# Gated linear attention and a cosine MLP in one kernel: four pairs' transposes moved to the DMA queue, and a new order of steps

## The chip, the cores and the metric

The kernel runs on one core of a Trainium2 chip. The metric is the device time of one execution in microseconds; lower is better. The engines in the profile are TensorE (PE, with its weight loads as PEld), VectorE (DVE), ScalarE (ACT), GpSimd (POOL) and SyncE (SP), which here only issues transfers; a name with q at its end (SPq, POOLq) is that engine's sequencer.

## The reference

Two layers follow each other. The first is a recurrence over 768 tokens, for 4 batches and 8 heads of width 48:

```python
for t in range(S):
    state = alpha[:, :, t, :, None] * state + np.einsum('bhd,bhe->bhde', k[:, :, t], v[:, :, t])
    y[:, :, t] = np.einsum('bhd,bhde->bhe', q[:, :, t], state)
x = y.transpose(0, 2, 1, 3).reshape(B * S, H * D)      # 3072 x 384
h = x @ w_in                                           # 384 x 2048
out = (h * np.cos(h)) @ w_out                          # 2048 x 384
```

Inputs and output are float32; the kernel computes its products in bfloat16.

## The kernel before

**Tiling.** The recurrence is computed in chunks. The 3072 tokens are cut into twelve blocks of 256 tokens, which the code calls J and this text a pair (each has two chunks of 128 tokens, c = 0 and 1; token parity is e). Three pairs make a batch, so the state starts anew at pairs 0, 3, 6 and 9. Within a pair, cumulative sums of log alpha give two factors: k is multiplied by the inverse of the running product and q by the product itself. After that the inner part is plain masked attention, and the state from earlier chunks is added.

**Steps of a pair.** `load a/k/q/v` bring the four inputs (384 KB each, on SP). `mula` multiplies the two tokens' alphas on POOL, `ln` takes logarithms on ACT, `cums` and `cums0` sum them on PE, `sub` is a subtraction on DVE, `icp` and `exps` are the exponentials on ACT; `eb` is all four exponentials of a pair with the next pair's `ln`. `sk` and `sq` scale k and q for one parity into the tiles kh and qh (on POOL, or on DVE where the order says `:D`). `castv` converts v on POOL, and `vst` stacks it into the tile vs with four SBUF-to-SBUF transfers of 64 KB on SP (L246); the first three pairs do that with `vpe` and `vev` on PE and ACT. `decay` prepares the chunk's decay on POOL. `trans` is 32 transposes on PE into PSUM (L288), and `evT` copies one chunk of them to the tile qkT in SBUF, on DVE or ACT (L294). `scores` (L303) are the products of k and q of one chunk, and `mask` (L309, DVE) masks them into SBUF. `outer` (L321), `add` (L335, DVE) and `state` (L343, POOL) update the state. `yT` (L370) forms the output of the pair, and `evy` (L379) copies a chunk of it to SBUF as xT.

**Steps of the MLP.** For each pair, `m1 u` (L390) is one of four steps of the first product: 12 matmuls of 256 columns into one two-bank PSUM tile. `sin u` (L396, ACT) is its cosine, `gate u` (L401, DVE) the product h cos h. The second stage is cut into parts: `m2 c part` (L419) is four matmuls of 384 columns into one PSUM bank, four parts make one chunk's 128 output rows. `evo` (L431) copies them to SBUF and `out` stores them from SP. The weights come in four quarters each, `w1 u` (L126) and `w2 u` (L132), cast to bfloat16 on the way and issued by POOL.

**Order.** Nothing is scheduled by the compiler: the table PLAN gives every step of every pair (the twelve columns) a number, and the program is emitted by these numbers. So each engine's queue is in the order of the table, and an engine that waits holds all that stands behind it on its queue; this is true of SP and of POOL, which issue transfers among other work. A colon and a letter after a number name the engine (D: DVE, A: ACT). IDLE lists dummy matmuls on PE, as (place, count).

**Buffers.** PSUM has three two-bank tiles named "h", which `cums0`, `vpe`, `trans`, `scores`, `outer`, `yT` and `m1` share; one bank "o" for `m2`, and one "x" for `cums`. In SBUF there are three buffers each for k, q, v, kh, qh, qkT, four for alpha, and two for vs. The ScalarE function table is loaded anew when exponentials and cosines alternate (nine times each way).

**Gate of the loads.** GATES makes the load of one input wait until a given step of TensorE is through. All loads that stand behind it on SP's queue wait as well:

```python
GATES, AFTER = {("a", 2): ("yT", 1)}, {}
```

Of the kernel before, what the change touches and what calls it, by code (L numbers as in the profile page):

```python
# [16 lines left out]
def kernel(  # L17
# [26 lines left out]
    NL, NQ, NV, NS = 4, 3, 3, 2  # L44
# [35 lines left out]
    for lst, nm, n in ((lna_t, "lna", NL), (kh_t, "kh", NQ), (qh_t, "qh", NQ), (vp_t, "vp", NV)):  # L80
        for r in range(n):
            t = consts.tile([C, 2, H, 64], BF, tag=f"{nm}{r}", name=f"{nm}{r}")
            nc.vector.memset(t[:, :, :, D:64], 0.0)
            lst.append(t)
# [14 lines left out]
    GATES, AFTER = {("a", 2): ("yT", 1)}, {}  # L99
# [7 lines left out]
    def load(nm, J):  # L107
        b, g = J // NJB, J % NJB
        t = sb.tile([C, H, 2, D], FP, tag=nm, name=nm, bufs=BUF["a" if nm == "a" else "in"])
        dma = nc.sync.dma_start(  # L110
# [120 lines left out]
    def scale_k(J, e, eng):  # L231
        icp_ = icp_sb.pop((J, e)).rearrange("p (h d) -> p h d", h=H)
        eng.tensor_tensor(out=kh_t[J % NQ][:, e, :, 0:D], in0=kqv["k", J][:, :, e], in1=icp_, op=ALU.mult)  # L233

    def scale_q(J, e, eng):
        cp = cp_sb[J, e][:, 0:HD].rearrange("p (h d) -> p h d", h=H)
        eng.tensor_tensor(out=qh_t[J % NQ][:, e, :, 0:D], in0=kqv["q", J][:, :, e], in1=cp, op=ALU.mult)  # L237
# [43 lines left out]
    def trans(J):  # L281
        T_ps[J] = ps.tile([C, 2, 2 * NP, 2, HC], BF, tag="h", name="T_ps", bufs=3)
        for i, x in ((1, kh_t[J % NQ]), (0, qh_t[J % NQ])):
            for p in range(NP):
                for e in range(2):
                    for c in range(2):
                        r = slice(HC * c, HC * c + HC)
                        last = nc.tensor.transpose(T_ps[J][:, c, i * NP + p, e, :],  # L288
                                            x[r, e, 2 * p : 2 * p + 2, :].rearrange("s h d -> s (h d)"), ident_bf[r, r])
# [23 lines left out]
    def outer(J):  # L313
# [3 lines left out]
        for p in range(NP):  # L317
            for e in range(2):
                for c in range(n):
# [3 lines left out]
                        kh[r, e, 2 * p : 2 * p + 2, :].rearrange("s h d -> s (h d)"),  # L323
# [61 lines left out]
    def mlp1(J, u):  # L385
        h_ps[J, u] = ps.tile([C, FW, T2], FP, tag="h", name="h_ps", bufs=3)
        for f in range(FW):
            ft = u * FW + f
            for kk in range(KT):
                nc.tensor.matmul(h_ps[J, u][:, f, :], w1[:, kk, ft * C : (ft + 1) * C], xT[J][:, kk, :],  # L390
                                 start=(kk == 0), stop=(kk == KT - 1))

# [15 lines left out]
    def mlp2(J, c, part):  # L408
# [8 lines left out]
        for o, cols in zip(o_ps[J, c], HALVES if last_tile else [slice(0, DM)]):  # L417
            for ft in fts:
                nc.tensor.matmul(o[:, 0 : cols.stop - cols.start], gsb[J][:, ft, c * C : (c + 1) * C], w2[:, ft, cols],  # L419
                                 start=(done == 1 and ft == fts[0]), stop=(done == MP and ft == fts[-1]))  # L420

# [19 lines left out]
    def idle(n):  # L441
# [5 lines left out]
    copies = {"DVE": nc.vector.tensor_copy, "ACT": nc.scalar.copy}  # L447
    mults = {"DVE": nc.vector, "POOL": nc.gpsimd}
    steps = {
        "load": lambda J, nm: load(nm, J), "w1": load_w1, "w2": load_w2,  # L450
# [4 lines left out]
        "evT": lambda J, c, eng="DVE": evict_T(J, c, copies[eng]), "scores": scores, "mask": mask, "outer": outer,  # L455
# [7 lines left out]
        "load a": "10 20 960 1030 1170 1450 1460 2230 2570 2290 3490 2960",  # L463
        "load k": "70 190 1040 1270 1530 2020 1990 3050 3500 4180 3440 4290",
        "load q": "100 230 300 1290 1620 1950 2580 2850 3980 4010 3970 4770",
        "load v": "40 290 1130 1220 1730 1930 1940 3090 3680 2990 4970 4850",
        "w1": "330 200 470 460 - - - - - - - -",
        "w2": "260 580 820 690 - - - - - - - -",
        "mula": "- - - 1090 1340 1790 2240 2480 3220 3070 3610 3820",
        "ln": "30 110 1060 1100 - - - - - - - -",  # L470
        "cums0": "50 160 1070 - - - - - - - - -",
        "cums": "140 210 1080 1120 1630 2130 2460 3140 3360 3830 4200 4660",
        "sub": "- - - 1200 1640 2140 2470 3150 3370 3840 4210 4950",
        "icp 0": "60 310 1180 - - - - - - - - -",
        "icp 1": "240 270 1330 - - - - - - - - -",
        "exps 0": "120 170 1140 - - - - - - - - -",
        "exps 1": "150 220 1230 - - - - - - - - -",
        "eb": "- - - 1430 1800 2250 2590 3230 3380 4150 4480 5190",
        "sk 0": "80:D 320 1190 1440 2180 2280 2940 3240 3650 4190 4490:D 5470",
        "sk 1": "250 280 1350:D 1560:D 2100 2260 2890:D 3340 3890 4510 4890 5480",  # L480
        "sq 0": "130:D 500:D 1150 1590 1910 2680 3130 3510 3990 4530 4800 5200",
        "sq 1": "340:D 510:D 1280:D 1670 1880 2270 2820 3530 4070 4520 4560 5450",
        "castv": "90 610 1210 1260 2120 2750 2720 3760 3730 4980 5000 5360",
        "vst": "- - - 1820 2320 3120 3110 4040 4450 5160 5010 5380",
        "vpe": "440 650 1540 - - - - - - - - -",
        "vev": "480:A 660:A 1580:A - - - - - - - - -",
        "decay": "180 730 1250 1470 2560 2450 3040 3810 3700 4780 4700 5210",
        "trans": "350 520 1360 1690 2190 2690 3160 3550 4350 4540 4900 5490",
        "evT 0": "370 590 1380 1840:A 2210 2700:A 3200 3710 4390:A 4550 4960:A 5500:A",
        "evT 1": "400:A 540 1520 1710 2380 2730 3180 3560 4420 4580 4910:A 5520",  # L490
        "scores 0": "380 600 1610 1890 2660 2830 3320 3960 4440 4930 5560 5760",
        "scores 1": "420 670 1570 1850 2390 3350 3480 4090 4460 5060 5080 5790",
        "mask 0": "410 640 1650 1900 2670 2860 3330 4000 4650 4940 5600 5770",
        "mask 1": "430 720 1600 1870 2420 3390 3540 4110 4470 5070 5100 5880",
        "outer": "360 680 1410 1700 2640 3170 3300 4120 4370 4990 5510 5780",
        "add 0": "390 710 1420 1720 2650 3190 3310 4130 4400 5040 5530 5840",
        "add 1": "620 760 - 1860 2800 - 3460 4250 - 5090 5700 -",
        "state 0": "450 750 1740 1810 2710 3400 3450 4140 4860 5050 5550 5960",
        "state 1": "630 990 - 2370 2810 - 3600 4360 - 5110 5830 -",
        "yT": "490 780 1750 2150 2790 3570 3620 4330 4870 5170 5670 5970",  # L500
        "evy 0": "530:D 790:D 1760:D 2160:D 2840:D 3590:D 3660:D 4380:D 4880 5180:D 5750 6030",
        "evy 1": "550 800 1770:D 2170:D 2900 3580 3630:D 4340 4920:D 5220:D 5710 6020",
        "m1 0": "740 940 2000 2520 2980 3670 3900 4620 5150 5610 5900 6040",
        "m1 1": "560 890 1960 2400 2950 3860 3750 4630 5250 5390 5850 6090",
        "m1 2": "860 920 2030 2310 3000 3690 4230 4710 5340 5930 6190 6290",
        "m1 3": "830 970 2050 2490 2910 3930 4080 4730 5580 5300 6230 6390",
        "sin 0": "770 1000 2010 2540 3010 3720 3910 4670 5230 5660 5910 6060",
        "sin 1": "570 900 1970 2410 2970 3870 3790 4690 5280 5400 5860 6100",
        "sin 2": "870 930 2040 2330 3080 3770 4270 4720 5350 5940 6200 6300",
        "sin 3": "840 1390 2060 2500 2920 4020 4220 4760 5620 5320 6240 6400",  # L510
        "gate 0": "810 1110 2070 2550 3030 3740 3920 4680 5240 5740 6070 6080",
        "gate 1": "700 910 1980 2440 3020 3880 3800 4740 5290 5420 5920 6110",
        "gate 2": "880 980 2110 2430 3210 3780 4280 4750 5370 5950 6210 6330",
        "gate 3": "850 1400 2340 2510 2930 4030 4260 4810 5630 5330 6310 6410",
        "m2 0 0": "1020 1490 2080 3060 3430 4310 4790 5410 5730 6130 6350 6510",
        "m2 0 1": "950 1480 2300 2880 3420 4170 4640 5270 5800 6140 6340 6540",
        "m2 0 2": "1050 1500 2200 2760 3470 4160 4820 5430 5810 6150 6360 6500",
        "m2 0 3": "1010 1510 2350 2770 3410 4300 4830 5440 5720 6120 6320 6550",
        "m2 1 0": "1300 1680 2610 3260 3950 4600 5030 5650 5980 6270 6420 6580",
        "m2 1 1": "1240 1780 2620 3280 4060 4430 5120 5570 6000 6250 6440 6590",  # L520
        "m2 1 2": "1310 1660 2600 3270 4050 4410 5130 5640 5990 6260 6460 6480",
        "m2 1 3": "1320 1830 2530 3250 3640 4570 5020 5590 5890 6220 6430 6490",
        "evo 0": "1160:D 1550 2360 3100:D 3520 4320 4840 5460 5820:D 6170 6370:D 6560",
        "evo 1": "1370:D 1920:D 2630:D 3290 4100:D 4610:D 5140:D 5680:D 6010:D 6280 6470:D 6600",
        "out 0": "2090 2780 3850 4590 3940 6160 5540 5870 6050 6180 6380 6570",
        "out 1": "2220 2740 2870 4500 4240 5310 5260 5690 6450 6520 6530 6610",
    }
    IDLE = [(45, 10), (155, 2), (345, 9), (375, 1), (435, 4), (485, 3)]
# [45 lines left out]
```

## Time and profile before

| | us |
|---|---|
| median of 3 runs (185.56 to 185.94) | 185.88 |
| the profiled execution | 185.78 |
| its span in the profile | 184.0 |
| TensorE busy | 173.0 (94% of the span) |
| VectorE busy | 134.5 (73%) |
| ScalarE busy | 124.9 (68%) |
| GpSimd busy | 83.5 (45%) |
| granted TensorE clock, mean | 0.999 |

All times are from one profiled execution. A group's line reads: line of the code, engine, operation, what it writes and reads, count, then busy time, mean duration in ns, and the idle time of the engine just before it with what ended that. The chain that ended last is followed back from the last instruction: each piece is what released the next one. A wait's line names who waited for whom, the total, how often and the longest. Landing times of single transfers are from the trace's DMA issues and the updates of their semaphores.

The first transfers of the execution were issued and landed as follows:

| transfer | queue | issued at | landed at |
|---|---|---|---|
| a, a, v, k, q, k, q (pairs 0 and 1) | SP | 0.74 to 7.21 | 4.41, 5.92, 7.43, 8.93, 10.44, 11.95, 13.41 |
| w1, step 1 | POOL | 8.55 | 15.30 |
| v of pair 1 | SP | 8.70 | 19.64 |
| q of pair 2 | SP | 10.18 | 26.43 |
| w1, steps 0, 3 and 2 | POOL | 13.99, 15.60, 16.40 | 22.15, 24.87, 27.10 |
| w2, first landed after that | POOL | 17.18 | 29.11 |
| a2, a3, k2, v2 | SP | 25.30 to 31.20 | 35.02, 36.32, 37.73, 39.07 |

### The profile page before, as it was taken

To read this page: it belongs to the slowest core of one execution; us is meant where nothing else is said; L and a number is where in the kernel's file an instruction comes from. 1 tells how busy PE (TensorE), PEld (TensorE's weight loads), DVE (VectorE), ACT (ScalarE), POOL (GpSimd) and SP (SyncE) were. 2 spreads that over 40 slices of the span, in tenths; PEclk is the share of its full clock that TensorE was granted. 3 is DMA by queue.
4 is the path that set the end of the run, shared out by engine and by line. 5 is a ranking of instruction groups with operands and counts; after the bars stand their busy time and mean duration, and the time that the engine had idled before them with its cause. 6 is when DMAs were issued, how large, how long until landed. Compare 5 with 4: busy or idle time off the path is not lost.

```text
span 184.0 us, 5742 instructions
## 1 busy us (share of the span) xinstructions
PE 173.0 (94%) x2457; PEld 125.5 (68%) x2458; DVE 134.5 (73%) x182; ACT 124.9 (68%) x157; POOL 83.5 (45%) x116
## 2 busy tenths in 40 slices
PE   7989579979999999999999999999899999999993
PEld 2445458646687776876787777876687677776672
DVE  7069777669999899799969898879587674734520
ACT  3745457789879999895978989869774517435201
POOL 5388550079883484939686093903901110000000
PEclk9999999999999999999999999999999999999999
DMA  6999999999999979963996579003420121010312
GB/s 146 261 248 224 216 202 206 262 256 257 261 213 262 304 170 278 260 164 85 278 289 154 140 215 245 18 6 88 143 71 4 41 88 51 0 43 4 127 44 86
DMA packets 60137, 29.47 MB, mean 160 GB/s; under 512 B 51024, under 2 KB 60112, under 8 KB 60112
## 3 DMA queue, kind: packets, MB, share of 16 engines
q1 hardware_dynamic: 56256, 25.86, 57.9%
q0 software_dynamic: 3712, 3.15, 10.6%
q8 instruction: 19, 0.31, 0.8%
q10 hardware_dynamic: 144, 0.10, 0.2%
q14 instruction: 6, 0.05, 0.1%
HBM read 25.17 MB, written 4.72 MB: 162 GB/s over the span
## 4 chain that ended last, share of the span: by engine, by line
PE 68%; DMA 11%; issue 7%; SPq 6%; POOL 5%; ACT 1%; DVE 1%; POOLq 0%; DVEq 0%
PE h_ps L390 28%; PE o_ps L419 26%; DMA v<-in_v_dram 6%; SPq L110 4%; PE y_ps L370 4%; DMA k<-in_k_dram 4%; PE A_ps L303 2%; PE T_ps L288 2%; PE U_ps L321 2%; SPq L246 2%; PE o_last L419 1%; DMA vs<-vp 1%; POOL un L343 1%; POOL a L154 1%; PE cums L168 1%
## 5 line engine op out<-in xcount | busy, mean ns | idle before, releaser
L401 DVE TENSOR_TENSOR gsb<-h_ps,c_sb 128x1024 bf16<-128x1024 f32 x48 | 58.4, 1222 | 20.0 <-ACT c_sb L396 18.8
L396 ACT ACTIVATE c_sb<-h_ps,halfpi 128x1024 bf16<-128x1024 f32 x48 | 53.4, 1114 | 28.5 <-PE h_ps L390 28.4
L390 PE MATMUL h_ps<-xT,w 128*128 128x256 bf16 x576 | 67.5, 273 | 0.7 <-DMA w<-in_moe_w_in_dram 0.5
L419 PE MATMUL o_ps<-w,gsb 128*128 128x384 bf16 x368 | 66.7, 326 | 0.0
L390 PEld LDWEIGHTS <-w 128*128 128x128 bf16 x576 | 55.4, 98 | 9.7 <-DMA w<-in_moe_w_in_dram 0.8
L419 PEld LDWEIGHTS <-gsb 128*128 128x128 bf16 x400 | 37.0, 98 | 20.8
L343 POOL TENSOR_TENSOR un<-us,c 128x384 bf16<-128x384 f32 x20 | 16.7, 836 | 33.1 <-DVE us L335 26.0
L309 DVE TENSOR_TENSOR A_sb<-A_ps,msk 128x1024 bf16<-128x1024 f32 x24 | 29.1, 1220 | 3.6 <-PE A_ps L303 3.4
L233 POOL TENSOR_TENSOR kh<-k,icp 128x384 bf16<-128x384 f32 x19 | 19.5, 1032 | 10.2 <-ACT lna L146 5.3
L237 POOL TENSOR_TENSOR qh<-q,cp 128x384 bf16<-128x384 f32 x19 | 18.8, 999 | 6.1 <-ACT cp L219 4.2
L154 POOL TENSOR_TENSOR a<-a 128x384 f32<-128x384 f32 x9 | 9.0, 997 | 11.8 <-DMA a<-in_alpha_dram 11.8
L240 POOL CAST vp<-v 128x768 bf16<-128x768 f32 x12 | 10.1, 853 | 6.4 <-DMA v<-in_v_dram 6.0
L146 ACT ACTIVATE lna<-a 128x768 bf16<-128x768 f32 x12 | 10.1, 842 | 4.1 <-DMA a<-in_alpha_dram 2.4
L141 ACT ACT_TABLE_LOAD x9 | 11.5, 1283 | 0.9 <-PEq L558 0.7
L294 DVE COPY qkT<-T_ps 128x1024 bf16<-128x1024 bf16 x17 | 11.4, 682 | 0.8 <-PE T_ps L288 0.8
L396 ACT ACT_TABLE_LOAD x9 | 11.5, 1283 | 0.2
L431 ACT COPY o_sb<-o_ps 128x384 f32<-128x384 f32 x10 | 4.8, 478 | 9.6 <-PE o_ps L419 9.6
L431 DVE COPY o_sb<-o_ps 128x384 f32<-128x384 f32 x13 | 7.2, 554 | 4.3 <-PE o_ps L419 4.2
L445 PE MATMUL idle_ps<-zeros 128*128 128x512 bf16 x28 | 9.0, 469 | 1.2 <-DVE halfpi L77 1.2
L379 DVE CAST xT<-y_ps 128x384 bf16<-128x384 f32 x14 | 7.7, 584 | 3.1 <-PE y_ps L370 2.9
L335 DVE TENSOR_TENSOR us<-U_ps,un 128x384 f32<-128x384 f32 x16 | 8.8, 551 | 1.3 <-PE U_ps L321 1.2
L303 PE MATMUL A_ps<-qkT 48*128 48x128 bf16 x192 | 8.7, 217 | 0.6 <-DVE qkT L294 0.5
(68 smaller groups left out, 149.2 us busy)
## 6 DMA issues: line engine op xcount, KB each, us to landing
a<-in_alpha_dram SPq DMA_DIRECT2D x12, 384.0 KB, 6.0
v<-in_v_dram SPq DMA_DIRECT2D x12, 384.0 KB, 6.1
k<-in_k_dram SPq DMA_DIRECT2D x12, 384.0 KB, 6.0
q<-in_q_dram SPq DMA_DIRECT2D x12, 384.0 KB, 6.2
out_dram<-o_sb SPq DMA_DIRECT2D x23, 192.0 KB, 2.3
vs<-vp SPq DMA_DIRECT2D x36, 64.0 KB, 2.8
w<-in_moe_w_in_dram POOLq DMA_DIRECT2D x4, 384.0 KB, 8.7
w<-in_moe_w_out_dram POOLq DMA_DIRECT2D x4, 384.0 KB, 10.7
```

The costliest lines, as they stand in the source:

```text
L141: nc.scalar.preload_act_table_set("natural_log_exp_and_others")
L233: eng.tensor_tensor(out=kh_t[J % NQ][:, e, :, 0:D], in0=kqv["k", J][:, :, e], in1=icp_, op=ALU.mult)
L237: eng.tensor_tensor(out=qh_t[J % NQ][:, e, :, 0:D], in0=kqv["q", J][:, :, e], in1=cp, op=ALU.mult)
L294: ins = copy(out=qkT_sb[J][:, c], in_=T_ps[J][:, c].rearrange("r n e s -> r n (e s)"))
L303: last = nc.tensor.matmul(A_ps[J, c][:, a, p, :], qkT[r, c, NP + p, :], qkT[r, c, p, :], start=True, stop=True)
L309: nc.vector.tensor_tensor(out=A_sb[J][:, c].rearrange("s a p t -> s (a p) t"), in0=A_ps.pop((J, c)).rearrange("s a p t -> s (a p) t"), in1 ...
L343: nc.gpsimd.tensor_tensor(out=u, in0=U_sum.pop(n), in1=c2_sb[J][:, :, c].unsqueeze(3).to_broadcast([C, NP, 2, D]), op=ALU.mult)
L390: nc.tensor.matmul(h_ps[J, u][:, f, :], w1[:, kk, ft * C : (ft + 1) * C], xT[J][:, kk, :], start=(kk == 0), stop=(kk == KT - 1))
L396: nc.scalar.activation(out=c_sb[J, u], in_=h_ps[J, u], func=AF.Sin, bias=halfpi, scale=1.0)
L401: nc.vector.tensor_tensor(out=gsb[J][:, u * FW : (u + 1) * FW], in0=h_ps.pop((J, u)), in1=c_sb.pop((J, u)), op=ALU.mult)
L419: nc.tensor.matmul(o[:, 0 : cols.stop - cols.start], gsb[J][:, ft, c * C : (c + 1) * C], w2[:, ft, cols], start=(done == 1 and ft == fts[0 ...
L431: copy(out=t, in_=o_ps.pop((J, c))[0][:, 0:DM])
```

## The change

1. For pairs 8 to 11, `trans` and `evT` are gone. In their place stands the step `tr`: a DMA transpose issued by SP, which reads one chunk's 64 rows of kh or qh (64 x 512 bfloat16, 64 KB) and writes them transposed into qkT. There are four for each pair, 16 in all. For that, the tiles kh and qh hold both parities of a head pair side by side, for all pairs.
2. The tile vs has three buffers instead of two.
3. GATES no longer holds a2. It holds a, k, q and v of pair 3 and a of pair 4 until the last matmul of `m2 0 3` of pair 0.
4. PLAN and IDLE are new throughout. Pair 2's q and a are loaded ahead of all other inputs that follow pair 1's, and its k and v stand behind a3. The first weights stand behind `castv` of pair 1 on POOL's queue. IDLE has 41 dummy matmuls instead of 29.
5. `load` can name another queue, and `m1` and `m2` can be gates; the new table leaves all loads on SP.

```diff
-    NL, NQ, NV, NS = 4, 3, 3, 2
+    NL, NQ, NV, NS = 4, 3, 3, 3
...
-            t = consts.tile([C, 2, H, 64], BF, tag=f"{nm}{r}", name=f"{nm}{r}")
+            t = consts.tile([C, 2, H, 64] if nm in ("lna", "vp") else [C, H, 2, 64], BF, tag=f"{nm}{r}", name=f"{nm}{r}")
             nc.vector.memset(t[:, :, :, D:64], 0.0)
-            lst.append(t)
+            lst.append(t.rearrange("s (p e) a d -> s p e a d", p=NP) if nm in ("kh", "qh") else t)
...
-    GATES, AFTER = {("a", 2): ("yT", 1)}, {}
+    GATES, AFTER = {('a', 3): ('m2', 0, 0, 3), ('k', 3): ('m2', 0, 0, 3), ('q', 3): ('m2', 0, 0, 3), ('v', 3): ('m2', 0, 0, 3), ('a', 4): ('m2', 0, 0, 3)}, {}
...
+    def trans_dma(J, x, c):
+        if J not in qkT_sb:
+            qkT_sb[J] = sb.tile([C, 2, 2 * NP, C], BF, tag="qkT", name="qkT", bufs=BUF["qkT"])
+        r = slice(HC * c, HC * c + HC)
+        i, src_t = {"k": (1, kh_t), "q": (0, qh_t)}[x]
+        nc.sync.dma_start_transpose(
+            out=qkT_sb[J][:, c, i * NP : (i + 1) * NP, :].rearrange("r n (e s) -> r (n e) s", e=2),
+            in_=src_t[J % NQ][r].rearrange("s p e a d -> s (p e a d)"))
...
     PLAN = {
-        "load a": "10 20 960 1030 1170 1450 1460 2230 2570 2290 3490 2960",
-        "load k": "70 190 1040 1270 1530 2020 1990 3050 3500 4180 3440 4290",
-        "load q": "100 230 300 1290 1620 1950 2580 2850 3980 4010 3970 4770",
-        "load v": "40 290 1130 1220 1730 1930 1940 3090 3680 2990 4970 4850",
-        "w1": "330 200 470 460 - - - - - - - -",
-        "w2": "260 580 820 690 - - - - - - - -",
+        "load a": "20 10 630 980 1430 1690 1920 2270 2690 2230 3120 4260",
+        "load k": "110 240 1160 1450 1740 1900 2300 2840 2330 4130 4240 5280",
+        "load q": "140 390 490 1530 1750 2210 2350 2680 3690 3700 4630 5250",
+        "load v": "150 340 1200 1560 2180 2470 2660 3190 3380 4570 5030 5440",
+        "w1": "480 380 580 560 - - - - - - - -",
+        "w2": "1080 1010 1090 860 - - - - - - - -",
...
-        "ln": "30 110 1060 1100 - - - - - - - -",
+        "ln": "50 30 640 1250 - - - - - - - -",
...
-        "sk 0": "80:D 320 1190 1440 2180 2280 2940 3240 3650 4190 4490:D 5470",
-        "sk 1": "250 280 1350:D 1560:D 2100 2260 2890:D 3340 3890 4510 4890 5480",
-        "sq 0": "130:D 500:D 1150 1590 1910 2680 3130 3510 3990 4530 4800 5200",
-        "sq 1": "340:D 510:D 1280:D 1670 1880 2270 2820 3530 4070 4520 4560 5450",
-        "castv": "90 610 1210 1260 2120 2750 2720 3760 3730 4980 5000 5360",
-        "vst": "- - - 1820 2320 3120 3110 4040 4450 5160 5010 5380",
+        "sk 0": "120 250 1190:D 1580 2050 2240 3140 3560 3850 4270 4830 5630",
+        "sk 1": "200:D 460 1170:D 1470:D 2020 2370 2940 3260 3750 4230 4990 5550:D",
+        "sq 0": "220:D 430:D 1110 1540:D 1970 2220 2640 3330 3960 4640 4780 5510:D",
+        "sq 1": "180 400:D 1150 1550:D 2040 2290:D 2780 3400 3990 4620 5150 5570",
+        "castv": "190 350 1300 1650 2190 2770 3050 3920 4340 4740 5090 5790",
+        "vst": "- - - 1830 2320 3010 3060 4090 4590 5120 5230 5870",
...
-        "trans": "350 520 1360 1690 2190 2690 3160 3550 4350 4540 4900 5490",
-        "evT 0": "370 590 1380 1840:A 2210 2700:A 3200 3710 4390:A 4550 4960:A 5500:A",
-        "evT 1": "400:A 540 1520 1710 2380 2730 3180 3560 4420 4580 4910:A 5520",
-        "scores 0": "380 600 1610 1890 2660 2830 3320 3960 4440 4930 5560 5760",
-        "scores 1": "420 670 1570 1850 2390 3350 3480 4090 4460 5060 5080 5790",
+        "trans": "230 500 1270 1590 2060 2590 3170 3580 - - - -",
+        "evT 0": "260:A 530:A 1330 1600:A 2140:A 2620 3250 3600 - - - -",
+        "evT 1": "310:A 520 1350 1640 2070 2670 3280 3590 - - - -",
+        "scores 0": "270 610 1340 1820 2250 2790 3300 3970 4380 5060 5180 5880",
+        "scores 1": "320 680 1360 1670 2310 3440 3420 3800 4410 4800 5400 5850",
...
+        "state 0": "540 700 1610 1800 2610 3530 3270 4000 4660 4850 5390 5820",
...
-        "yT": "490 780 1750 2150 2790 3570 3620 4330 4870 5170 5670 5970",
+        "yT": "570 740 1630 2100 2740 3540 3500 4100 4730 5130 5520 5970",
...
-        "m1 1": "560 890 1960 2400 2950 3860 3750 4630 5250 5390 5850 6090",
-        "m1 2": "860 920 2030 2310 3000 3690 4230 4710 5340 5930 6190 6290",
+        "m1 1": "720 1130 1780 2810 2890 3640 3610 4530 4920 5530 6040 6140",
+        "m1 2": "840 930 1960 2410 2850 3790 4120 4490 4890 5830 5660 6050",
...
+        "gate 1": "770 1220 1890 2830 2910 3670 3630 4560 4970 5620 6230 6170",
+        "gate 2": "880 960 2030 2440 2880 3910 4190 4510 4940 6020 5690 6080",
...
+        "tr k 0": "- - - - - - - - 3860 4680 5140 5780",
+        "tr k 1": "- - - - - - - - 3870 4480 5210 5840",
+        "tr q 0": "- - - - - - - - 4280 4980 5170 5860",
+        "tr q 1": "- - - - - - - - 4400 4650 5190 5580",
     }
-    IDLE = [(45, 10), (155, 2), (345, 9), (375, 1), (435, 4), (485, 3)]
+    IDLE = [(35, 10), (55, 3), (225, 9), (265, 5), (315, 6), (405, 4), (495, 3), (605, 1)]
```

## The prediction

> **What bounds the kernel now.** I read the page's engine table first, then the busy time by stage, TensorE's waits, and the chain that ended last.
>
> ```profile
> PE 173.0 (94%) x2457; PEld 125.5 (68%) x2458; DVE 134.5 (73%) x182; ACT 124.9 (68%) x157; POOL 83.5 (45%) x116
> ...
> L294 DVE COPY qkT<-T_ps 128x1024 bf16<-128x1024 bf16 x17 | 11.4, 682 | 0.8 <-PE T_ps L288 0.8
> ...
> vs<-vp SPq DMA_DIRECT2D x36, 64.0 KB, 2.8
> ```
>
> By stage (window, its length, then busy time of each engine, granted clock, DMA share, GB/s):
>
> ```profile
> 0.00:27.15 27.15, 21.41 (x324) 12.44 (x326) 18.06 (x46) 13.83 (x20) 17.06 (x36) 1.00 1.14 216
> 27.15:52.00 24.85, 23.55 (x327) 16.63 (x328) 18.97 (x24) 20.93 (x29) 12.93 (x15) 1.00 1.15 247
> 52.00:108.00 56.00, 56.00 (x830) 43.11 (x830) 50.02 (x60) 48.26 (x60) 35.94 (x44) 1.00 0.89 217
> 108.00:151.00 43.00, 42.18 (x700) 31.34 (x699) 33.53 (x41) 29.14 (x36) 16.77 (x22) 1.00 0.31 82
> ```
>
> TensorE idles 1.3 us between 27 and 52, nothing to 108, 0.8 after that. Its waits:
>
> ```profile
> PE cums L168 <- ACT lna L146: 1.0, 1, 1.0
> PE y_ps L370 <- DMA vs<-vp: 0.8, 1, 0.8
> ```
>
> The chain's late part, from the pairs whose transposes are replaced:
>
> ```profile
> 109.21 0.57 PE T_ps L288 x32
> ...
> 112.08 0.47 PE T_ps L288 x32
> ...
> 122.95 0.57 PE T_ps L288 x32
> ...
> 126.81 0.59 SPq L246
> 127.41 0.04 issue
> 127.45 2.55 DMA vs<-vp
> 130.00 0.04 issue
> 130.04 0.75 PE y_ps L370 x32
> ...
> 138.74 0.57 PE T_ps L288 x32
> ```
>
> The reader sees a TensorE-bound kernel from 27 us on, in which a late transpose is on the path itself; only a start of 27 us is bound by transfers and short chains. The sum is made against the profiled execution: span 184.0, time 185.78, so 1.78 outside the span; the median is 185.88.
>
> **The change part by part.**
>
> *Transposes of pairs 8 to 11 leave TensorE:* 0.57 + 0.47 + 0.57 + 0.57 = 2.18 us, from a stage without slack. The product step behind a transpose took 0.76 instead of 0.65, so up to 4 x 0.11 more may go: 2.18 to 2.62, and I take 2.18, which is shown. Their eight evictions (four on ACT at 1.01, four on DVE at 0.68) count nothing, being under TensorE.
>
> *Sixteen DMA transposes on SP.* None is in the trace. From below the nearest row is `vs<-vp`: the same 64 KB, SBUF to SBUF, same queue, 0.59 to issue, 2.0 to 2.8 to land. From above a 384 KB load: 1.45 to issue, 4.83 at the longest (a k load at 26.34), 6.0 to land. I take 0.59 and 2.6, by bytes and route. 16 x 0.59 = 9.4 us of SP, which issued nothing from 111.7 to 122.99. To see the slack I sum TensorE's new order back from the last matmul, 180.85, with chain durations (first-stage step 1.31, second-stage part 0.65, scores 0.33, y 0.90). Pair 8: its q transposes stand behind three loads (4.5 us) and land near 109; scores at 113.8. Pair 9: 7 us to spare. Pair 10 is tight: outer of pair 9 ends at 123.3, `mask 1` and `add 0` on DVE at 125.4, then POOL in its order: `state 0` 126.3, `sk 1 J10` 127.3, `castv` 128.1, `sq 1 J10` 129.1; the k transpose is issued at 127.3, the q one at 129.1, landing at 132.3 for scores at 133.8: 1.5 us to spare. Behind them on SP wait `vst J10` and the loads of q and k of pair 11. Pair 11: its exponentials end at 137.2, its scales on DVE and POOL between 140 and 143.5, so q goes at 142 and k from 143.5, four issues, landed by 148; scores at 150.6, and `vst J11` lands by 151 for y at 153.8. A landing of 6.0 instead of 2.6 costs 1.9 at pair 10. I take +0.3, between 0 and 1.9.
>
> *A third `vs` buffer:* the queue's wait for y of pair 8 at 122.95 goes, and with it TensorE's 0.8 at 130. Next late is `vst J10`, behind four transposes, landed at 136.6 for y at 140.2. -0.8, at worst 0. The third buffer's memset (0.31 on POOL at 3 us, first use at 7.5) is free.
>
> *Start.* The first seven landings now come at 4.41, 5.92, 7.43, 8.93, 10.44, 11.95, 13.41; the new order puts a1, a0, k0, q0, v0, k1, v1 there, then q1 14.9, q2 16.4, a2 17.9 at the same pace. POOL issues the first w1 quarter only behind `castv 1`, at 14.25 (now 8.55); alone a quarter takes 2.0 (27.10 to 29.11), so it lands between 18.7 and 21.0 (the latter with the 6.75 that it takes now), the fourth by 24.6 to 26.9. Meanwhile, with the rows' durations (a scale 0.56 on DVE and 1.0 on POOL, mask and gate 1.22, y eviction 0.59, sine 1.11, `state` 0.84): scales of pair 0 to 10.45, transposes 11.05, ACT evictions 12.1 and 13.6, DVE masks 13.8 and 15.5, add 16.05, both q scales of pair 1 17.15, transposes 17.5, evictions 18.9, y of pair 0 18.0 to 18.8, its DVE eviction 20.0, `mask 0 J1` 21.2, first-stage step 1 at 21.25, `mask 1 J1` 22.95, y of pair 1 23.85, two evictions on DVE 25.05, `gate 1 J0` 26.27, step 2 of pair 0 at 26.55. Now the same step, with the same work behind it, starts at 27.15: -0.6. Twelve more idle matmuls (0.22 each) fall into waits.
>
> *From there to 52.* Only a2 and q2 really go ahead of the weights: k2 and v2 are issued behind a3, which waits for a product at 30.9. By today's landings behind the weights (35.02, 36.32, 37.73, 39.07) they come no later than now, and DVE reaches k2 only at 38.2. ACT switches its table twice round pair 2's exponentials (1.28 + 1.9 + 1.28), so `gate 2 J1` ends at 35.75, and DVE then runs without a break to 51. Following the queues I find that TensorE waits 0.45 for `gate 3 J0` (28.95), 0.3 for `gate 2 J1`, 0.15 for `evo 0 J0` (37.2), 0.35 for the k scales of pair 2 (39.5), 0.15 and 0.35 for its two evictions (41.4, 42.1), 0.4 for the q scales of pair 3 (46.1) and 0.7 for `mask 1 J2` (47.3): 2.85 against 1.3 now. -0.6 + 1.55 = +0.95; the same walk counted by work done gives -0.1, as it omits the changes between kinds of matmul (1.2 us in this stage now), which fall into the waits. I take +0.4, between -1.0 and +1.0.
>
> *52 to 91:* walked on in the same way, TensorE waits for `ln J5` (0.4), then for PSUM banks until `gate 3 J2` (0.25), `evo 0 J2` (0.4), `gate 0 J3` (0.2) and `add 1 J4` (0.25) are through, and for `mask 1 J5` (0.25): 1.75, where none is now. I take +0.6, between 0 and 1.75, for the same reason. From 154 on the order is like today's, no change. The new layout of kh and qh keeps 384 elements per scale: nothing, either way under TensorE.
>
> Sum: -2.18 - 0.8 + 0.4 + 0.6 + 0.3 = -1.7, and 185.78 - 1.7 = **184.1 us**.
>
> **The rivals.**
>
> *The transposes clog SP (slower).* Each issue of x us delays all behind it. Pair 11's chain 143.5 + 3x plus four `vst` issues (2.4) and a landing (2.6) must be done by 153.8: it decides at x = 1.8, three times the `vs` row, and each us above costs 3 there; scores 10 fail from 2.2. At 3 us that is +3.6 and about +1: 188.7; at the longest issue shown, 4.83, it is +9 at pair 11 alone, over 193. For it: nothing bounds x but rows of another kind; against it: the `vs` row. The Trainium skill's page "DMA: Bandwidth & Descriptors" speaks for this rival: its table of cycles before and after gives 262,144 for 8,192 SBUF-to-SBUF tiles, and its list of DMA operations calls a tile 256 B, so 64 KB would be an estimated 6.8 us of issue at 1.2 GHz. "Advanced Engine Details and Errata", X-Bar Transpose, says instead that such transfers are as fast as ordinary ones, by which the sum stays as it is; no run here shows either.
>
> *a2 is late (slower).* `ln J2` stands before the first sine on ACT. A landing at L ends that sine at L + 0.84 + 1.28 + 1.11, and its gate can start at 25.05: it decides at 21.8, and each us later is a us. Beside weights two loads took 6.2 (v1, to 19.64) and 6.8 us (q2, to 26.43). If only a2 is caught, it lands near 23 (+1.2, 185.3); if q2 is too, near 27.6 (+5.8, 189.9). Against it: now loads keep their pace until 13.41, 3.9 us after the first quarter's issue ends; 15.15 + 3.9 is past 17.9. The Trainium skill ("DMA: Bandwidth & Descriptors", Queues, rings and completion order) has engines alternate between queues packet by packet, which would catch q2 and a2; the trace agrees only after 13.41.
>
> *The waits eat the gain (no change).* All walked waits real, +0.95 and +1.75: 184.1 + 0.55 + 1.15 = 185.8. For it: DVE is at 89% from 52 to 108 already; against: today's order has as many tight spots and waits for none.
>
> *Dense:* no waits and the larger saving, -0.6 - 2.62 - 0.8: 181.8.
>
> **How the numbers follow.** Forecast 0.55 (its own range 182.6 to 185.4), dense 0.07, no change 0.13, clogged SP 0.12, late a2 0.13. Under and over 0.2% (0.37 us, about what can be told from no change): faster 0.55 + 0.07 = 0.62; same 0.10 of the no-change case; slower 0.03 + 0.12 + 0.13 = 0.28. The range 181.9 to 187.5 leaves out most of the clogged case, half of the late one and the end of the dense one, about 0.2.
>
> **What would show it.** Right: no `T_ps` group for the last four pairs, TensorE idle under 1 us after 91, `vs` gone from its waits, step 2 of pair 0 near 26.6, transposes issued in under 1.8 and landed in under 4. Wrong: long SPq rows at the transposes or A_ps waiting for them; the first sine after 24; TensorE waiting over 5 us between 27 and 91.

## The result and the profile after

The changed kernel takes 183.39 us (median of 4 runs, 183.16 to 183.56) against 185.91 us for the kernel before beside it: a ratio of 0.987, with a 95% interval of 0.9854 to 0.9887. It is faster, by 1.3%. The profiled execution took 183.31 us with a span of 181.5; before, it was 185.78 and 184.0.

The page of the changed kernel, its engines and its DMA issues:

```profile
PE 172.4 (95%) x2339; PEld 123.6 (68%) x2342; DVE 129.4 (71%) x174; ACT 123.9 (68%) x159; POOL 82.5 (45%) x115
...
vs<-vp SPq DMA_DIRECT2D x36, 64.0 KB, 3.1
```

The same stages as before (window, its length, busy time of each engine, granted clock, DMA share, GB/s), of the changed kernel:

```profile
0.00:27.15 27.15, 22.33 (x334) 12.93 (x337) 17.20 (x44) 15.78 (x22) 19.04 (x38) 1.00 1.12 210
27.15:52.00 24.85, 23.77 (x336) 17.26 (x337) 19.05 (x25) 21.56 (x31) 10.21 (x13) 1.00 1.10 228
52.00:108.00 56.00, 55.95 (x870) 42.36 (x868) 48.30 (x58) 48.88 (x62) 37.27 (x46) 1.00 0.97 211
108.00:151.00 43.00, 43.00 (x549) 31.23 (x546) 33.91 (x38) 27.39 (x34) 15.98 (x21) 1.00 0.69 152
```

TensorE has no idle time left from 108 to 151, where it had 0.8 us. The DMA share of that stage went from 0.31 to 0.69: loads, stackings and the transposes now lie there. The longest waits of TensorE that are left in the changed kernel (total, times, longest), apart from its first instruction:

```profile
PE cums_h L168 <- ACT lna L146: 0.8, 2, 0.4
PE o_ps L431 <- DMA w<-in_moe_w_out_dram: 0.8, 1, 0.8
PE h_ps L401 <- DVE A_sb L320: 0.8, 1, 0.8
PE y_ps L381 <- POOL un L354: 0.6, 1, 0.6
PE h_ps L401 <- DMA w<-in_moe_w_in_dram: 0.4, 1, 0.4
```

The line `y_ps <- vs` is gone. Two lines stand for weights, both before 37 us. In the kernel before, y of pair 9 waited at 130.04: SP held pair 10's stackings until y of pair 8 had read their buffer, at 122.95, and pair 9's stood behind them. SP's waits of the kernel before show it:

```profile
SPq L246 <- PE y_ps L370: 11.7, 2, 11.2
```

The chain of the changed kernel at y of pair 8:

```profile
118.91 0.90 PE y_ps L381 x56
119.81 0.45 PE U_ps L332 x16
120.25 0.23 PE A_ps L314 x8
120.48 1.41 PE o_ps L431 x8
121.89 3.93 PE h_ps L401 x36
```

No `T_ps` step and no SP or DMA piece is left there. Y of pair 8 ends at 119.81, where it ended at 122.95, and pair 9's stackings are issued from 117.58, ahead of that end, where they were issued from 126.17. The transposes themselves (instances, then issue time least, median, most in ns, first and last start), from the group of the tile qkT after 88 us:

```profile
L298 SPq DMA_TRANSPOSE qkT<-kh x8: 1207/1262/2353, 91.0 to 142.6; - x8
L298 SPq DMA_TRANSPOSE qkT<-qh x8: 1193/1262/1964, 100.4 to 143.9; - x8
```

One issue holds SP for 1.26 us at the median, against 0.59 for a `vst` of the same 64 KB. They land 2.6 to 5.0 us after their issue begins, 3.1 at the median.

**Where the time went.** TensorE's last matmul ends at 178.39 instead of 180.85: 2.46 us. Up to 52 us the two kernels are level: the first step of pair 2's first stage starts at 49.53, and with the two pieces that the old order already had behind it (1.95 + 0.33) that is 51.81, against 51.98 before. So 2.3 of the 2.5 us come after 52. I also split TensorE's time from 27.1 us on by the tile it works for, counting from the start of one matmul to the start of the next, idle time apart: `T_ps` 5.45 to 3.58 us, idle 2.10 to 1.12, all else together 0.4 more (it changes its kind of product ten times more often). -1.87 - 0.98 + 0.4 is the whole difference.

### The profile page after: what moved, and what is told of

Its sections match the earlier page's. It is cut to its first block, busy times and chain, and to the rows that moved or that the text cites. A ratio compares the mean times of both kernels' runs of the same rounds, so it can differ in the third digit from the quotient of the medians.

```text
span 181.5 us, 5505 instructions
## 1 busy us (share of the span) xinstructions
PE 172.4 (95%) x2339; PEld 123.6 (68%) x2342; DVE 129.4 (71%) x174; ACT 123.9 (68%) x159; POOL 82.5 (45%) x115
## 3 DMA queue, kind: packets, MB, share of 16 engines
q0 software_dynamic: 3712, 3.15, 11.6%
## 4 chain that ended last, share of the span: by engine, by line
PE 70%; DMA 9%; ACT 5%; POOL 4%; SPq 3%; issue 3%; DVE 3%; ACTq 0%
PE o_ps L431 28%; PE h_ps L401 28%; DMA w<-in_moe_w_out_dram 6%; PE y_ps L381 5%; SPq L110 3%; DMA v<-in_v_dram 3%; PE A_ps L314 3%; PE U_ps L332 2%; PE o_last L431 1%; DVE A_sb L320 1%; ACT L141 1%; POOL un L354 1%; POOL w L132 1%; PE T_ps L290 1%; ACT lna L146 1%
## 5 line engine op out<-in xcount | busy, mean ns | idle before, releaser
L401 PE MATMUL h_ps<-xT,w 128*128 128x256 bf16 x576 | 68.5, 273 | 1.3 <-DVE A_sb L320 0.8
L408 ACT ACTIVATE c_sb<-h_ps,halfpi 128x1024 bf16<-128x1024 f32 x48 | 52.8, 1114 | 20.8 <-PE h_ps L401 20.6
L238 POOL TENSOR_TENSOR qh<-q,cp 128x384 bf16<-128x384 f32 x17 | 17.2, 1024 | 13.0 <-ACT cp L219 10.0
L390 ACT CAST xT<-y_ps 128x384 bf16<-128x384 f32 x12 | 6.7, 594 | 11.4 <-PE y_ps L381 11.3
L444 ACT COPY o_sb<-o_ps 128x384 f32<-128x384 f32 x12 | 5.7, 479 | 11.3 <-PE o_ps L431 11.3
L458 PE MATMUL idle_ps<-zeros 128*128 128x512 bf16 x38 | 10.8, 426 | 1.5 <-DVE halfpi L77 1.2
L444 DVE COPY o_sb<-o_ps 128x384 f32<-128x384 f32 x11 | 6.1, 555 | 4.8 <-PE o_ps L431 4.7
L390 DVE CAST xT<-y_ps 128x384 bf16<-128x384 f32 x12 | 6.6, 586 | 2.1 <-PE y_ps L381 1.9
```

Of the source, the lines that this page charges most:

```text
L238: eng.tensor_tensor(out=qh_t[J % NQ][:, :, e, :, 0:D], in0=kqv["q", J][:, :, e].rearrange("p (n a) d -> p n a d", a=2), in1=cp.rearrange(" ...
L390: ins = copy(out=xT[J][:, :, c * C : (c + 1) * C].rearrange("r i (t e) -> r i e t", e=2), in_=y_ps[J][:, c, 0 : KT * C].rearrange("r (i e ...
L401: last = nc.tensor.matmul(h_ps[J, u][:, f, :], w1[:, kk, ft * C : (ft + 1) * C], xT[J][:, kk, :], start=(kk == 0), stop=(kk == KT - 1))
L408: nc.scalar.activation(out=c_sb[J, u], in_=h_ps[J, u], func=AF.Sin, bias=halfpi, scale=1.0)
```

## The experiments

Theory A, the prediction's: each part has a price of its own. The transposes give what TensorE no longer does, the third buffer gives the `vs` wait, and the new order by itself costs a little. Theory B: the new order alone pays. Theory C, the clogged queue: the DMA transposes pay only where nothing urgent stands behind them on SP.

**1. The new order with transposes on TensorE** (`order_pe`): the 16 DMA transposes go out; `trans` and its evictions come back for pairs 8 to 11, just ahead of their scores, and one scale of pair 10's q moves up to be done by then.

```diff
-        "trans": "230 500 1270 1590 2060 2590 3170 3580 - - - -",
+        "trans": "230 500 1270 1590 2060 2590 3170 3580 4325 4685 5101 5745",
...
-        "tr k 0": "- - - - - - - - 3860 4680 5140 5780",
+        "tr k 0": "- - - - - - - - - - - -",
```

> The changed kernel with the 16 DMA transposes taken out again: pairs 8 to 11 are transposed on TensorE and evicted as before the change, each a few steps ahead of its scores; all else stays. Theory (transposes pay): the 2.18 us of TensorE work come back into a stage without slack, so about 185.5, which is 2.1 slower than the changed kernel (183.4) and 0.4 faster than before. Rival (the new order pays): the transposes are small change and the time stays at 183.4 to 183.9.

Measured: 187.20 us, a ratio of 1.0068 (1.0043 to 1.0092). Theory B falls, as far as this placing of the transposes goes: without the DMA transposes the new order is slower than the old kernel. But A missed too, as the transposes are worth 3.8 us here and not 2.2. Split as above, `T_ps` rose by 2.32 us (3.58 to 5.90), the other products by 1.06 and idle time by 0.54. Part of that is my own placing: in the chain of this kernel both evictions of pair 10 stand on ScalarE ahead of xT, and TensorE waits for one of them (the first line is from its waits):

```profile
PE A_ps L314 <- ACT qkT L305: 0.4, 1, 0.4
```

```profile
132.10 0.59 PE T_ps L290 x32
...
132.72 1.93 ACT qkT L305 x2
134.64 0.96 ACT xT L390 x2
...
135.65 1.47 PE h_ps L401 x12
```

**2. The old order with all 16 DMA transposes** (`old_order_dma`): PLAN, IDLE, GATES and two `vs` buffers as before; the four `tr` steps of a pair stand where its scales end.

```diff
-        "trans": "350 520 1360 1690 2190 2690 3160 3550 4350 4540 4900 5490",
+        "trans": "350 520 1360 1690 2190 2690 3160 3550 - - - -",
...
+        "tr k 0": "- - - - - - - - 4071 4531 4892 5481",
+        "tr q 0": "- - - - - - - - 4072 4532 4891 5482",
+        "tr k 1": "- - - - - - - - 4073 4533 4893 5483",
+        "tr q 1": "- - - - - - - - 4074 4534 4894 5484",
```

> The old order, gate and two vs buffers, with DMA transposes for pairs 8 to 11, issued as soon as the scales of a pair are done. Theory (transposes pay): 185.9 - 2.2 = 183.7, if the issues of 1.26 us that the trace of the changed kernel shows delay no stacking of v on SP by more than its slack. Rival (the new order pays): 185.9 or slower.

Measured: 194.58 us, a ratio of 1.0471 (1.0415 to 1.0527). Its waits and a part of its chain:

```profile
PE A_ps L314 <- DMA qkT<-qh: 4.5, 1, 4.5
PE y_ps L381 <- DMA vs<-vp: 4.4, 2, 4.1
```

```profile
120.88 1.90 SPq L298
...
122.89 1.21 SPq L298
...
124.15 1.26 SPq L298
...
125.46 1.26 SPq L298
...
126.77 4.05 DMA v<-in_v_dram
...
130.97 0.84 POOL vp L242
...
131.83 0.47 SPq L248
...
136.18 2.00 DMA vs<-vp
...
138.31 0.88 PE y_ps L381 x27
```

This is the clogged queue in one view: four transposes, behind them a load of v, behind that its cast on GpSimd, then eight stackings on SP, then y. The condition of the theory did not hold. The two waits are 8.6 us of the loss; in the stage that holds them, from 108 to 151 us, the granted clock was 0.92 where it was 1.00, so some of the rest is TensorE running slower behind them.

**3 and 4. The third buffer in each order.** `new_ns2` is the changed kernel with two `vs` buffers, `old_ns3` the kernel before with three.

```diff
-    NL, NQ, NV, NS = 4, 3, 3, 3
+    NL, NQ, NV, NS = 4, 3, 3, 2
```

> The changed kernel with two vs buffers instead of three. As the prediction had it (the third buffer takes TensorE's wait of 0.8 us away): 183.4 + 0.8 = 184.2. Rival (the new order alone does it, since the stacking of pair 10 is now issued at 130.5, long after y of pair 8 at 119.8): unchanged, 183.4.

> The kernel before with three vs buffers, nothing else. If the third buffer is what lifts the wait for y of pair 8: the eight stacking transfers are no longer issued at 122.99 but some us earlier, TensorE's wait of 0.8 us at 130 goes, 185.1. If another step holds the queue: 185.9.

Measured: `new_ns2` 183.78 us, ratio 0.9878 (0.9837 to 0.9919), not to be told from the changed kernel; `old_ns3` 184.34 us, ratio 0.9909 (0.9878 to 0.994), which is 1.4 us better than the 185.74 of the kernel before in the same runs. The third buffer pays in the old order, more than the 0.8 us of its wait: between the two traces, 1.10 us are gained from the end of pair 8's y to the end of pair 9's, and 0.36 lie ahead of that, where no run shows that the buffer is the cause. In the new order no gain from it shows: y of pair 8 is done by 119.8 and the next stackings are issued from 130.48.

**5. Each DMA transpose twice** (`tr_double`): a second transpose of the same rows into a tile that nothing reads follows each, which is extra work for SP's queue and for the transfers, and none for a computing engine.

```diff
+        nc.sync.dma_start_transpose(
+            out=spare[:, len(spare_used) % 8].rearrange("r n (e s) -> r (n e) s", e=2),
+            in_=src_t[J % NQ][r].rearrange("s p e a d -> s (p e a d)"))
+        spare_used.append((J, x, c))
```

> The changed kernel, each DMA transpose issued a second time, into a spare tile that nobody reads, so SP is held for 2 x 1.26 = 2.5 us at each of the 16. The prediction's price of a slow issue: pair 11 loses 3 us for each us above 1.8, so 3 x 0.7 = 2.1, and pair 10 some 0.6 above 2.2: 186.1. If the loads of pair 11's q, k and v, which stand behind pair 10's transposes, come late as well (5 us), up to 190. Rival (SP's time is free, whatever the transposes take): 183.4.

Measured: 197.9 us, a ratio of 1.0607 (1.0556 to 1.0657). The direction is that of the clogged queue, the size was missed by far: 16 spare issues of 1.27 us are 20 us of SP, and the kernel is some 14 us slower. Not all of that is the queue itself: the granted clock was 0.96 from 108 to 151 us and 0.88 from 151 to 178.5, where the changed kernel had 1.00. The waits name the queue (this profile is of an execution of 200.08 us, so its sizes are a little large):

```profile
PE A_ps L319 <- DMA qkT<-qh: 5.9, 3, 3.2
PE o_ps L436 <- DVE o_sb L449: 2.1, 1, 2.1
PE A_ps L319 <- DMA qkT<-kh: 1.8, 2, 0.9
```

**6. The third pair's `a` after the weights** (`a2_late`): one more gate in the changed kernel.

```diff
-    GATES, AFTER = {('a', 3): ('m2', 0, 0, 3), ...
+    GATES, AFTER = {('a', 2): ('yT', 0), ('a', 3): ('m2', 0, 0, 3), ...
```

> The changed kernel, with a2 held back on SP until the last y matmul of pair 0 (19.2 us) instead of going at 11.7, so that it lands beside the weights. The prediction's price: free up to a landing at 21.8, then one us for each us. Beside the weights it should land at 26 to 29, so +4 to +7: 187.5 to 190.5. Rival (the start is bound by the weights, which now have the queue to themselves from 16.5 on): within 0.5 of 183.4.

Measured: 193.98 us, a ratio of 1.044 (1.0404 to 1.0477). The chain:

```profile
19.27 12.50 DMA a<-in_alpha_dram
...
33.95 1.12 ACT c_sb L408
35.08 0.02 issue
35.10 1.24 DVE gsb L413
...
36.38 2.72 PE h_ps L401 x12
```

Beside the weights the 384 KB load took 12.5 us. The prediction's price of this rival (free up to a landing at 21.8, then a microsecond each) gives 31.77 - 21.8 = 10.0 us; 10.6 came. The landing itself was misjudged: 26 to 29 was expected, and so 190.5 us at most. And that 10.0 and 10.6 are so near is in part luck. In this trace (of an execution of 194.84 us) the first-stage step that waits starts 9.2 us later than in the changed kernel, 36.38 against 27.17, and y of pair 2 is 11.6 late: the other 2.4 come behind the gap, where the granted clock was 0.50 from 36.35 to 40 us. In the changed kernel a2 lands at 19.18, so the rival did not come about, with 2.6 us to spare.

**7. The first weights earlier** (`w_early`): in the changed kernel, the first quarter of w1 is issued on POOL's queue behind the cast of pair 0's v instead of pair 1's, and the others move up.

```diff
-        "w1": "480 380 580 560 - - - - - - - -",
+        "w1": "355 195 560 480 - - - - - - - -",
```

> The changed kernel with the first w1 quarter issued behind castv of pair 0 (about 11.6 us instead of 14.35) and the second behind castv of pair 1, in place of the first; the other two keep their places or come one scale earlier. If the start is bound by the weights (TensorE waits 0.43 us for a w1 quarter at 27.2 and 0.79 for a w2 quarter at 36.2): 183.4 - 1.2 = 182.2. Rival (loads and weights share the engines, so what the weights gain, v1, q1 and a2 lose): 183.4 to 186, with a2 landing after 21.8.

Measured: 182.18 us, a ratio of 0.9793 (0.9759 to 0.9826): the fastest of all, 1.2 us below the changed kernel. The four quarters land at 19.15, 21.98, 23.89 and 25.87 instead of 20.91, 23.34, 25.21 and 27.12; both waits for weights, 0.43 and 0.79 us, are gone. Now a2 lands at 20.73, later than 19.18 but still ahead of 21.8, and no wait of TensorE comes of it. Steps of pair 0's first stage now follow y of pair 1 without a gap (`w_early`, chain):

```profile
22.73 0.96 PE y_ps L381 x56
23.70 2.75 PE h_ps L401 x24
```

Its longest waits, again apart from the first instruction:

```profile
PE h_ps L401 <- DVE A_sb L320: 0.8, 1, 0.8
PE y_ps L381 <- POOL un L354: 0.6, 1, 0.6
PE cums_h L168 <- ACT lna L146: 0.4, 1, 0.4
PE h_ps L401 <- DVE gsb L413: 0.3, 1, 0.3
```

**8. The old order, three buffers, DMA transposes for pairs 8, 9 and 11** (`old_mix`): the second experiment without the pair whose scores waited.

```diff
-    NL, NQ, NV, NS = 4, 3, 3, 2
+    NL, NQ, NV, NS = 4, 3, 3, 3
...
-        "tr k 0": "- - - - - - - - 4071 4531 4892 5481",
+        "tr k 0": "- - - - - - - - 4071 4531 - 5481",
```

> The old order with three vs buffers and DMA transposes for pairs 8, 9 and 11 alone; pair 10, whose scores the old order puts right behind its transposes, stays on TensorE. Theory (transposes pay wherever their scores stand far enough behind): 184.3 (old order with three vs buffers) - 3 x 0.55 = 182.7, without a wait of A_ps for a DMA. Rival (DMA transposes pay in the new order alone): 184.3 or slower.

Measured: 189.60 us, a ratio of 1.0224 (1.0172 to 1.0275): a miss by 7 us. The scores no longer wait, but y does:

```profile
PE y_ps L381 <- DMA vs<-vp: 4.1, 2, 3.8
```

Pair 9's four transposes stand on SP from 110.33 to 117.4, and the last two loads of v go out behind them at 118.58 and 119.31. With the same three buffers and no DMA transposes (`old_ns3`) they went out at 109.80 and 110.43. They land by 124.93, and the stackings start at 125.83 instead of 119.21. Behind the longer wait the clock falls here too: 0.96 granted from 108 to 151 us.

**9. The same with three loads moved** (`old_mix_v`): the last loads of v and q go ahead of pair 9's transposes on SP's queue. Nothing else differs from the eighth.

```diff
-        "load q": "100 230 300 1290 1620 1950 2580 2850 3980 4010 3970 4770",
-        "load v": "40 290 1130 1220 1730 1930 1940 3090 3680 2990 4970 4850",
+        "load q": "100 230 300 1290 1620 1950 2580 2850 3980 4010 3970 4525",
+        "load v": "40 290 1130 1220 1730 1930 1940 3090 3680 2990 4524 4523",
```

> This is the former run (old order, three vs buffers, DMA transposes for pairs 8, 9 and 11, pair 10 on TensorE) with one thing moved: the last two loads of v and the last of q stand ahead of pair 9's transposes on SP's queue instead of behind them. Theory (a transpose on SP's queue costs what is queued behind it; with nothing urgent behind it, it pays what TensorE leaves out): the v loads are issued at about 109 to 111 us as in the kernel before, the stackings of vs at about 123, the wait of y_ps for vs (4.1 us) goes, and the time falls from 189.6 to 182.7 us (the old order with three buffers, 184.34, less three pairs at 0.55). Part of the gain may stay out if pair 9's transposes, now 2 us later, reach the scores of pair 9 late: up to 184.3. Rival (the transposes need the new order, or cost TensorE time by other means than the queue, such as memory traffic): 186 us or more, with the vs wait or a new one in its place.

Measured: 183.27 us, a ratio of 0.9869 (0.9838 to 0.99). The stackings are issued from 120.21, the wait for `vs` is gone, and the chain has TensorE alone where the eighth had SP and DMA pieces:

```profile
120.71 0.90 PE y_ps L381 x56
121.61 0.57 PE T_ps L290 x32
122.18 0.23 PE A_ps L314 x8
122.41 0.01 issue
122.42 0.52 PE U_ps L332 x16
```

Three places in a queue's order were worth 6.3 us, the clock lost behind the wait included. And the old order, with three buffers and twelve of the sixteen DMA transposes, is as fast as the changed kernel (183.39). The new order is therefore not needed as such: what is needed is that nothing urgent stands behind the transposes.

## Why the prediction was right, point by point

The forecast of 184.1 us was 0.7 above the measured 183.39, on the right side and inside its own range; none of the three rivals with a price above it came true. The saving was where the prediction had put it, on TensorE; that the sum came so near is in part luck, as errors of both signs cancel. The terms:

- **Transposes off TensorE, -2.18.** Right in kind. The `T_ps` time fell by 1.87 and all other products grew by 0.4: about -1.5 net between the two traces. The price depends on what stands beside it. It was 3.8 us between `order_pe` and the changed kernel, of which `T_ps` was 2.32. It was 1.07 for three pairs between `old_ns3` and `old_mix_v` (184.34 to 183.27), where I expected 1.65. In the traces of the latter two `T_ps` fell by 1.52 (5.45 to 3.93); y of pair 2 is level (48.66 and 48.65), and the last matmul ends 1.45 earlier (179.37 to 177.92). So TensorE gained nearly all of it. Behind the last matmul `old_mix_v` takes 0.26 longer, which no run explains. The new layout of kh and qh, which comes with the transposes, shows no price: a scale of k on GpSimd takes 1.04 us in `old_ns3` and 1.03 in `old_mix_v`.
- **Sixteen DMA transposes, +0.3.** The issue time of 0.59 us, taken from the `vs` row as nearest by bytes and route, failed: 1.26 was measured, more than twice. The bounds, 0.59 to 4.83, held it, and so did the point from which the clogged queue decides (1.8). The cost was 0: no scores wait for a transpose. Pair 10's first chunk had its transposes by 128.51, and its scores ran at 130.82; the second chunk had them by 131.16, and its scores ran at 134.22. The walk had put the landing at 132.3 and the scores at 133.8. One sign that the prediction named failed: landings came up to 5.0 us after the issue, not under 4.
- **The third `vs` buffer, -0.8.** The wait went, but the buffer was not what removed it. `new_ns2` shows that the new order with two buffers has no such wait either. The step named the wrong part of the change: here the order removed the wait. In the old order, the kernel with the third buffer is 1.4 us faster, and the traces put 1.10 at this wait.
- **The start, -0.6.** This failed. Step 2 of pair 0's first stage ran at 27.17, not 26.55. The work ahead of it was in time; the last quarter of w1 landed at 27.12, past the upper end (26.9) of the landing the step gave, and TensorE waited 0.43 for it. `w_early` shows that the weights were the limit: with that quarter at 25.87 the wait is gone.
- **To 52, +0.4 with the start.** Measured -0.17 at equal work. The total is 0.6 better although the start in it was 0.6 worse than said. Of the eight waits listed, 2.85 us in all, one shows in the trace: `mask 1 J2`, 0.2 at 47.69 instead of 0.7 at 47.3. The longest wait of the stretch, 0.79 at 36.17 for a quarter of w2, stood in no term.
- **52 to 91, +0.6.** Measured: 0.05 us idle in the whole stage from 52 to 108. The walk by hand gave 1.75, and none of its six waits came. Why the walk finds waits that do not come is not shown; that median durations leave no room for an engine to catch up is my reading. Against the terms as put, the stretch to 52 came out 0.6 better, this one 0.6 and the DMA transposes 0.3, while the transposes taken off TensorE gave 0.7 less: 0.8 better in all, against the 0.7 between forecast and measurement.

**The clogged queue** was a real rival, with 1.26 against its threshold of 1.8. Its price was too low: 3 us for each us above at pair 11 counts one pair only, and `tr_double` paid some 14 for 1.27 more at each transpose, with the clock lost behind its waits in it. The Trainium skill's page "DMA: Bandwidth & Descriptors" gave an estimated 6.8 us of issue, from its table of cycles and its list of operations; the trace does not agree, at 1.26. The Trainium skill's page "Advanced Engine Details and Errata", X-Bar Transpose, says that such transfers are as fast as ordinary ones; the trace does not agree either, at 1.26 against 0.59 to issue the same 64 KB. The issue lay between the two.

**The late a2** was priced near (10.0 against 10.6, in part by luck, as the sixth experiment says), and a2 landed at 19.18 with the threshold at 21.8. The landing was forecast at 17.9: it came 1.3 later, 2.65 us behind the load ahead of it (16.53), where the loads before had landed 1.5 apart, and the first quarter of w1 was on its way by then. The rule of the Trainium skill ("DMA: Bandwidth & Descriptors", Queues, rings and completion order) that engines alternate between queues packet by packet fits the 12.5 us that the load takes in `a2_late` when issued in the middle of the weights.

What stays open: how much of `order_pe`'s 3.8 us beyond its 2.32 of `T_ps` is due to my placing of the evictions, and how much of its gain the new order owes to each of the other steps it moves.

## What to carry to other kernels

An operation moved to a DMA queue costs what stands behind it there: before counting what the compute engine saves, list the loads and copies queued behind the new issue and who waits for them at the end of that chain. Here the same sixteen or twelve transposes gave 194.6, 189.6 or 183.3 us, and three moved loads made the last difference. Where a part of a change is credited with removing a wait, run the change without that part: the third buffer was credited, and the order had done it.

## What the runs showed of the hardware

- A DMA transpose of 64 KB within SBUF holds SP for 1.26 us, a plain copy of 64 KB for 0.59. With SP free they land 1.3 us apart, which is the pace of the issues: in the changed kernel, issued at 125.93, 127.17 and 128.49, they landed at 128.51, 129.83 and 131.16. Where they queued behind loads (`old_mix_v`) they landed closer, at 119.48, 119.85, 120.34 and 121.12. Plain copies queued likewise in the changed kernel landed at 121.62, 121.81, 121.99 and 122.16. So in these two rows the transfer is slower too, by some 2 to 4 times, but with SP free it is the issue that sets the pace.
- In these runs a long gap on TensorE cost more than its length. In `a2_late`, the granted clock of the stage from 27 to 52, which has the 8.7 us gap, averaged 0.79, where it was 1.00, and the first step after it took 2.72 us instead of 1.48. The stages with the long waits of `old_order_dma` (4.5 and 4.1 us), `old_mix` (3.8) and `tr_double` (3.2) had 0.92, 0.96 and 0.96. How long a gap must be is not shown: in the first 27 us of `old_ns3` the clock was 0.94 with no wait over 1.5 us. The rows of `a2_late`:

```profile
PE h_ps L401 <- DVE gsb L413: 8.7, 1, 8.7
```

```profile
27.15:52.00 24.85, 16.12 (x139) 11.36 (x137) 10.52 (x11) 16.94 (x19) 4.29 (x6) 0.79 0.83 151
```
